# A power-of-two scale from one matmul sum of 128 maxima, and a new order table, in an attention and two-MoE kernel

## The chip, the cores and the metric

The kernel runs on one core of a Trainium2 chip. The metric is the time of one execution on the device in microseconds (us). The engines are TensorE (PE: matmuls and transposes), VectorE (DVE), ScalarE (ACT), GpSimd (POOL) and SyncE (SP, which issues the DMAs). Each engine works through its own queue in order; semaphores tie the queues together.

## The reference

Banded attention feeds a first MoE layer with a SoLU activation and a layer norm, and that feeds a bilinear MoE layer. Cut to what matters:

```python
def _attn_ref(q, k, v):                 # (4, 8, 576, 64)
    scores = scale * np.matmul(q, k.transpose(0, 1, 3, 2))
    # heads 0-3: a local band of 32; heads 4-7: every 32nd position
    attn = softmax(np.where(masks, scores, -1e9))
    return np.matmul(attn, v)

x = attn_out as (2304, 512)
h = x @ w_in                            # 512 -> 1024
solu = h * softmax(h)
ln = (solu - mu) / np.sqrt(var + 1e-06) * g_ln
x = ln @ w_out                          # 1024 -> 512
return (x @ w_a) * (x @ w_b) @ w_out2   # 512 -> 1536 -> 512
```

The inputs of the weights are float64, which the kernel turns into float32 on the chip.

## The kernel before

The work has two stages that overlap little. In the first (0 to some 290 us) PE interleaves the attention of four batches with the first MoE layer, 128 tokens a tile, 18 tiles. In the second it computes the bilinear layer in blocks of 768 tokens, as a seven-product (Strassen-like) scheme of float16 pairs, high part and low part.

**Attention.** Per pair of heads, `group_T` transposes q and k on PE into the PSUM ring `s` (L608), ACT copies them out (L615, L618). `att_tile` puts the mask and the scores into `s` (L696, L701), DVE takes the negated maximum (L719) and adds it (L728), ACT exponentiates (L731), DVE sums (L732) and takes the reciprocal (L736, L738), POOL multiplies (L777 or L768). Batch 0 is "direct": PE transposes the result into `y` (L764), ACT copies it as `PT` (L774), and P@V (L798) uses float32 values. Batches 1 to 3 split P and V into float16 high and low parts (P: L784, L785; V: `group_v`, L644 on ACT and L647 on DVE), transpose P by DMA (L786), and do P@V in three passes (L803 to L805). P@V writes the PSUM tile `xbank`, from which ACT copies to `xT` (L825).

**The values' scale.** Before V is split, it is scaled by a power of two. `pair_scale` takes for each of two head pairs the largest absolute value of every partition (L630, DVE, into a column of `am`) and calls `pow2_scale`: PE transposes `am` into `xbank` (L500), DVE reduces (L501), PE transposes the two maxima (L505), DVE reduces (L506), three tiny DVE ops make the power of two and its inverse in one row (L511 to L513), PE broadcasts the row to all partitions by a matmul with ones (L515), and DVE multiplies by units (L516). This runs six times, twice in each of batches 1 to 3. `scale_wout` uses the same function once for w_out (eight columns), and the second stage three times.

**The shared bank.** `xbank` is one PSUM tile of 512 columns. P@V uses the columns up to 352 as ring `x`, the scale those from 352 on as ring `scp`. The two rings know nothing of each other in the plan, but the program's semaphores follow the tile as a whole: a transpose of the scale waits for ACT's copy out of it, and P@V for the scale's last reads.

**The first MoE layer.** `moe1(t)`: ACT and DVE split a slice of `xT` into `xh` and `xl` (L845, L849), PE makes `h` in 24 matmuls (L856), DVE takes the maximum (L861), ACT exponentiates (L862), POOL makes a reciprocal (L867 to L869), DVE multiplies (L871, into `wk`), and the rest (L875 to L890) normalises. `h` is one PSUM buffer, so tile t+1 cannot start before L871 of tile t. `s2` multiplies by `wout` (L910) into `y`. The weights come as float64, 512 KB a piece, and are converted by ACT and DVE (`from_f64`, L455, L461, L465); `split_wout` (L524, L526) needs the scale of w_out. `scale_ab` (L929) sums norms by a matmul of a 128x128 block of ones by two columns.

**The order.** `Plan.op` collects operations with engines, costs in microseconds, and dependences; `schedule` puts them out in the order of the table `ISSUE`, which was found beforehand by a search that reads these costs and the rings' buffers. Within an engine the table's order is the queue's order, and no engine passes over a waiting instruction. The costs are read by the search alone.

## Time and profile before

| | us |
|---|---|
| median of 3 runs | 700.77 (699.4 to 700.79) |
| profiled execution | 695.03 |
| its span, first to last instruction | 693.3 |
| PE busy | 664.4 (96%) |
| DVE busy | 571.5 (82%) |
| ACT busy | 447.2 (65%) |
| POOL busy | 144.7 (21%) |

The mean granted clock of TensorE over the span is 0.994. The share of DMA engines busy is near 1 up to 60 us and falls afterwards. Busy times are shares over a span with different stages, so they are read by stretch. Each wait is put down to whatever came last. The rows that matter stand in a section of their own below.

### The profile page before, as it was taken

How to read it: one execution, taken by the hardware profiler on the slowest of the kernel's cores; microseconds unless marked ns; L12 is line 12 of the kernel's file. 1: busy time of each engine (PE TensorE's matmuls, PEld its weight loads, DVE VectorE, ACT ScalarE, POOL GpSimd, SP SyncE). 2: the span in 40 equal slices, each digit the busy share in tenths (PEclk: the TensorE clock that was granted, in tenths of full speed). 3: DMA queues.
4: the chain of work that ended last, by engine and by line, in shares of the span. 5: the costliest groups of instructions: out<-in, count | busy, mean ns of one | idle time of the engine just before them, and what ended most of it. 6: DMA issues, size and time to landing. Idle time of an engine off the chain costs nothing.

```text
span 693.3 us, 15572 instructions
## 1 busy us (share of the span) xinstructions
PE 664.4 (96%) x5991; PEld 498.8 (72%) x5991; DVE 571.5 (82%) x1238; ACT 447.2 (65%) x898; POOL 144.7 (21%) x268
## 2 busy tenths in 40 slices
PE   5987899999999999999999999999999999999997
PEld 4766677878787888886576676766767676775676
DVE  5789899789678644999999999799977989786576
ACT  3679868777767644986978787676543746434421
POOL 5544546536537432410000000000000000000000
PEclk9999899999999999999999999999999999999999
DMA  9999979999998434677254043653522304641023
GB/s 209 258 243 244 188 138 194 264 186 268 222 248 199 102 81 102 188 249 240 103 184 152 0 141 104 198 201 97 175 100 94 120 32 166 237 138 46 1 92 122
DMA packets 152650, 109.68 MB, mean 158 GB/s; under 512 B 101376, under 2 KB 131072, under 8 KB 152576
## 3 DMA queue, kind: packets, MB, share of 16 engines
q1 hardware_dynamic: 152576, 108.69, 60.4%
q8 instruction: 47, 0.77, 0.5%
q14 instruction: 27, 0.22, 0.1%
HBM read 65.41 MB, written 27.53 MB: 134 GB/s over the span
## 4 chain that ended last, share of the span: by engine, by line
PE 61%; DVE 8%; ACT 5%; issue 1%; POOL 0%; ACTq 0%; POOLq 0%
PE N L1326 17%; PE M L1326 13%; PE N L1472 9%; PE y L910 7%; PE M L1472 7%; PE h L856 6%; ACT y L1267 1%; DVE p L1423 1%; ACT w L1128 1%; DVE w L1132 1%; DVE y L1269 1%; DVE A L1415 1%; DVE A L1393 1%; DVE V L647 0%; ACT Z L1238 0%
## 5 line engine op out<-in xcount | busy, mean ns | idle before, releaser
L1326 PEld LDWEIGHTS <-w 128*128 128x128 f16 x1512 | 147.9, 98 | 91.7 <-issue 2.0
L1326 PE MATMUL N<-y,w 128*128 128x384 f16 x864 | 156.2, 326 | 0.7 <-ACT N L1333 0.7
L1472 PEld LDWEIGHTS <-p 128*128 128x128 f16 x1071 | 104.7, 98 | 20.4 <-issue 1.1
L1326 PE MATMUL M<-y,w 128*128 128x384 f16 x648 | 118.5, 326 | 0.8 <-ACT N L1333 0.8
L910 PE MATMUL y<-lnT,wout 128*128 128x256 f16 x864 | 101.4, 273 | 1.5 <-DMA lnT<-ln 0.8
L910 PEld LDWEIGHTS <-wout 128*128 128x128 f16 x864 | 82.0, 98 | 15.2 <-issue 4.1
L1418 ACT CAST p<-A 128x384 f16<-128x384 f32 x119 | 59.2, 512 | 40.1 <-DVE A L1393 22.6
L856 PE MATMUL h<-win,xh 128*128 128x512 f32 x288 | 79.8, 417 | 2.7 <-DVE wk L871 2.6
L1472 PE MATMUL N<-wo,p 128*128 128x256 f16 x612 | 77.7, 273 | 1.0 <-DVE yst L1488 1.0
L856 PEld LDWEIGHTS h<-win,xh 128*128 128x128 f32 x288 | 54.4, 198 | 14.4 <-DVE wk L871 3.3
L1423 DVE TENSOR_TENSOR p<-A,p 128x384 f16<-128x384 f32 x119 | 62.3, 552 | 2.7 <-ACT p L1418 2.7
L1472 PE MATMUL M<-wo,p 128*128 128x256 f16 x459 | 60.2, 273 | 0.0
L455 ACT ACTIVATE f64f<-raw 128x512 f32<-128x512 f32 x52 | 34.6, 674 | 11.2 <-DMA raw<-in_moe_w_in_dram 7.3
L856 PE MATMUL h<-win,xl 128*128 128x512 f32 x144 | 39.2, 394 | 0.0
L1415 DVE TENSOR_TENSOR A<-A 128x384 f32<-128x384 f32 x72 | 39.0, 553 | 0.2
L1488 DVE SCALAR_TENSOR_TENSOR ob<-M,osc,ob 128x256 f32<-128x256 f32 x63 | 27.8, 477 | 12.6 <-PE M L1472 11.1
L777 POOL TENSOR_TENSOR e<-e,r 128x324 f32<-128x324 f32 (+2 forms) x30 | 26.2, 881 | 50.0 <-DVE r L738 28.2
L861 DVE TENSOR_REDUCE st<-h 128x1 f32<-128x1024 f32 x18 | 22.0, 1220 | 17.2 <-PE h L856 17.1
L856 PEld LDWEIGHTS h<-win,xl 128*128 128x128 f32 x144 | 26.7, 188 | 5.9
L465 DVE SCALAR_TENSOR_TENSOR f64f<-f64f,raw 128x512 int32<-128x512 int32 x36 | 28.8, 804 | 2.3 <-ACT f64f L455 1.8
L1348 ACT COPY V<-M 128x384 f32<-128x384 f32 x36 | 17.0, 473 | 20.0 <-PE M L1326 19.9
L871 DVE SCALAR_TENSOR_TENSOR wk<-h,st,wk 128x1024 f32<-128x1024 f32 x18 | 23.0, 1279 | 7.8 <-POOL st L869 7.7
(191 smaller groups left out, 1207.0 us busy)
## 6 DMA issues: line engine op xcount, KB each, us to landing
raw<-in_moe_w_out_dram SPq DMA_DIRECT2D x20, 512.0 KB
o_scr<-ob SPq DMA_DIRECT2D x36, 256.0 KB
ob<-o_scr SPq DMA_DIRECT2D x30, 256.0 KB
raw<-in_moe_w_a_dram SPq DMA_DIRECT2D x12, 512.0 KB
raw<-in_moe_w_b_dram SPq DMA_DIRECT2D x12, 512.0 KB
y_scr<-y SPq DMA_DIRECT2D x14, 384.0 KB
y<-y_scr SPq DMA_DIRECT2D x14, 384.0 KB
y_scr<-ys SPq DMA_DIRECT2D x18, 256.0 KB
```

The costliest lines, as they stand in the source:

```text
L455: act(0.67, lambda: nc.scalar.activation(f(), raw()[:, :, 1].bitcast(F32), AF.Prelu, scale=2.0 ** -112, alpha=-2.0 ** 32), (raw,), (f,))
L465: dve(0.77, lambda: nc.vector.scalar_tensor_tensor(g().bitcast(I32), f().bitcast(I32), 3, raw()[:, :, 0], op0=ALU.logical_shift_left, op1= ...
L777: pool(0.1 + 1.2 * pl, lambda: nc.gpsimd.tensor_tensor(ev(), ev(), r()[:, :ng].unsqueeze(2).to_broadcast([128, ng, nk]), op=ALU.mult), (r, ...
L856: nc.tensor.matmul(h()[:, 512 * n:512 * n + 512], xs[xa]()[:, kk], win[wa][:, kk, 512 * n:512 * n + 512], start=(pi == 0 and kk == 0), sto ...
L871: dve(1.3, lambda: nc.vector.scalar_tensor_tensor(e(), h(), st()[:, 7:8], e(), op0=ALU.mult, op1=ALU.mult, accum_out=st()[:, 2:3]), (h, (s ...
L910: nc.tensor.matmul(y()[:, 256 * mi:256 * mi + 256], wout[:, kk, wa, 128 * m:128 * m + 128], lnT()[:, xa, kk], start=(pi == 0 and kk == 0), ...
L1326: nc.tensor.matmul(to()[:, :HB], w()[:, wa, a, kk], y7[b]()[:, xa, kk], start=first and pi == 0 and kk == 0, stop=pi == 2 and kk == 1, ski ...
L1415: dve(TD, lambda: nc.vector.tensor_tensor(to(), x(), y(), op=op), toks, (to,))
L1418: act(0.5, lambda: nc.scalar.copy(pu(0, a), x()), (x,), (pu.tok(0, a),))
L1423: dve(TD, lambda: nc.vector.tensor_tensor(pu(1, a), x(), pu(0, a), op=ALU.subtract), (x, pu.tok(0, a)), (pu.tok(1, a),))
L1472: nc.tensor.matmul(bk(i), pus[u](xa, a)[:, 128 * tt:128 * tt + 128], wo()[:, u, b, wa], start=a == A11 and u == 0 and pi == 0, stop=u == U ...
L1488: dve(0.475, lambda: nc.vector.scalar_tensor_tensor(dst(), bk(i), s(), dst(), op0=ALU.mult, op1=ALU.add), (src, osc), (obt(t, c),))
```

## The change

Five things change.

1. `pair_scale` no longer calls `pow2_scale`. It multiplies a 128x128 block of ones by each column of `am`, adding up in one PSUM column (`total`): every partition then holds the sum of all 128 maxima of both head pairs instead of the largest. DVE masks the sum to its exponent (one op on 128x1), and `powers` makes the inverse and the scale in three ops on 128x1.
2. Ring `scp` is gone. `x` is the whole of `xbank`, one buffer, which P@V, the values' scale and the scale of w_out take in turn; the plan therefore orders them.
3. `scale_wout` keeps its seven steps, but takes its tile from `x` (`scp="x"` in `PARAM`).
4. Costs of PE operations that the search reads are raised.
5. The table `ISSUE` is a new one: 3237 operations instead of 3261, with rows moved on every engine.

```diff
-PARAM = dict(back=12, first=40, early=(0,), seed=4, noise=0.1, direct=((0, 0), (0, 1)), stay=0.0, pf1=(),
+PARAM = dict(scp="x", back=12, first=40, early=(0,), seed=4, noise=0.1, direct=((0, 0), (0, 1)), stay=0.0, pf1=(),
 ISSUE = [int(n) for n in """
-10 0 13 11 14 5 2 15 16 1 12 6 18 17 21 8 35 19 9 20 7 4 22 414 37 430 3 771 787 36 39 38 40 43 41 42 181 187 23 66 44
+10 0 13 5 14 2 15 1 11 16 12 6 17 18 20 8 35 21 9 19 414 7 4 22 426 3 763 37 775 36 39 38 40 43 41 42 181 187 24 23 66
...
-    ring("psR", "x", None, F32, 1).fixed = lambda n: xbank[:, :352]
-    ring("psR", "scp", None, F32, 1).fixed = lambda n: xbank[:, 352:]
+    ring("psR", "x", None, F32, 1).fixed = lambda n: xbank
...
-    def pow2_scale(am, toks, n, unit, dst, dtok, top=14, least=60, ps="scp", sm=""):
-        tp = bank(ps) if ps == "M" else rings[ps].new()
+    def pow2_scale(am, toks, n, unit, dst, dtok, top=14, least=60, ps=None, sm=""):
+        tp = bank(ps) if ps == "M" else rings[ps or pm["scp"]].new()
-        pe(0.12, lambda: nc.tensor.transpose(tp()[:n, :128], am(), ident), (*toks, "ident"), (tp,))
+        pe(0.2, lambda: nc.tensor.transpose(tp()[:n, :128], am(), ident), (*toks, "ident"), (tp,))
...
-        pe(0.1, lambda: nc.tensor.matmul(tp()[:, 144:146], ones, row()[:1], start=True, stop=True), (row, "small"), (tp,))
+        pe(0.25, lambda: nc.tensor.matmul(tp()[:, 144:146], ones, row()[:1], start=True, stop=True), (row, "small"), (tp,))
...
-            pe(NM * 0.09, transposes, ((raw, 0), (raw, 1), "ident"), (tp,), 855)
+            pe(NM * 0.09 + 0.05, transposes, ((raw, 0), (raw, 1), "ident"), (tp,), 855)
...
-        pow2_scale(am, (am,), len(gs), 0, sc, sc)
+        tp, m1 = rings["x"].new(), rings["m1"].new()
+
+        def total():
+            for i in range(len(gs)):
+                nc.tensor.matmul(tp()[:, :1], ones_sq, am()[:, i:i + 1], start=i == 0, stop=i == len(gs) - 1)
+        pe(0.3, total, (am, "small"), (tp,))
+        dve(0.15, lambda: nc.vector.tensor_scalar(m1().bitcast(I32), tp()[:, :1].bitcast(I32), 0x7F800000, None,
+                                                  op0=ALU.bitwise_and), (tp,), (m1,))
+
+        def powers():
+            up, down = sc()[:, 0:1], sc()[:, 1:2]
+            nc.vector.tensor_scalar(down, m1(), 2.0 ** -14, 2.0 ** -60, op0=ALU.mult, op1=ALU.max)
+            nc.vector.reciprocal(up, down)
+            nc.vector.tensor_scalar(down, down, 1.0 / PSCALE, None, op0=ALU.mult)
+        dve(0.4, powers, (m1,), (sc,))
...
-            pe(nblk * 0.14, transposes, (tok, "ident"), (pt,), nblk * rows * 2)
+            pe(nblk * 0.15 + 0.05, transposes, (tok, "ident"), (pt,), nblk * rows * 2)
...
-                s1_ops.append(pe(4 * 0.230, mm, [xs[xa]] + [((("win", kk, n), wa)) for kk in range(4)], (h,), 2048))
+                s1_ops.append(pe(4 * 0.237, mm, [xs[xa]] + [((("win", kk, n), wa)) for kk in range(4)], (h,), 2048))
...
-        pe(0.12, lambda: nc.tensor.matmul(tp()[:, :2], ones_sq, fro[:, u, m], start=True, stop=True),
+        pe(0.22, lambda: nc.tensor.matmul(tp()[:, :2], ones_sq, fro[:, u, m], start=True, stop=True),
```

Three places show how the queues change. Line numbers of the new kernel differ: L635 is the matmul of `total`, L637 DVE's masking of the sum, and L499 to L514 are the old L501 to L516 shifted by two; L883 is the old L871 (eviction of `h`), L873 the old L861, L888 the old L876, L868 the old L856.

On DVE, the last rows ahead of the eviction of `h` of MoE tile 1. Before:

```order
L736 SCALAR_TENSOR_TENSOR sm_927<-sm_927,over 128x6
L465 SCALAR_TENSOR_TENSOR wout<-f64f,raw_797 128x512
L461 TENSOR_SCALAR raw_869<-raw_869 128x512
L738 RECIPROCAL r<-sm_927 128x6
L861 TENSOR_REDUCE st<-h 128x1
L465 SCALAR_TENSOR_TENSOR wout<-f64f,raw_869 128x512
L732 TENSOR_REDUCE sm_1013<-e_116 128x6
L849 TENSOR_TENSOR xl<-xT,xh 128x512
L719 TENSOR_REDUCE mx<-s 128x6
L871 SCALAR_TENSOR_TENSOR wk,st<-h,st,wk 128x1024
```

The same place in the changed kernel:

```order
L888 SCALAR_TENSOR_TENSOR ln<-wk,st,ln 128x1024
L873 TENSOR_REDUCE st<-h 128x1
L504 TENSOR_REDUCE m_1086<-xbank 1x1
L744 TENSOR_REDUCE sm_1088<-e_114 128x6
L509 TENSOR_SCALAR m_1086<-m_1086 1x1
L510 TENSOR_SCALAR row<-m_1086 1x1
L511 RECIPROCAL row<-row 1x1
L861 TENSOR_TENSOR xl<-xT,xh 128x512
L744 TENSOR_REDUCE sm_1111<-e_115 128x6
L514 TENSOR_TENSOR wsc<-xbank,units 128x2
L748 SCALAR_TENSOR_TENSOR sm_1088<-sm_1088,over 128x6
L883 SCALAR_TENSOR_TENSOR wk,st<-h,st,wk 128x1024
```

The steps of the scale of w_out, which stood behind this eviction, now stand ahead of it. From one eviction to the next (tile 0 to tile 1) 18 DVE rows stood between, now 32 instructions do.

On PE, the first values' scale. Before, it follows the last matmuls of MoE tile 2, with its second transpose behind two groups of other work and its broadcast 20 rows further on:

```order
L856 MATMUL h<-win_108,xl 128x512 x4
L608 MATMUL s<-ident,rawq 128x96 x6
L500 MATMUL xbank<-ident,am 2x128
L798 MATMUL xbank<-PT,rawl 64x64 x2
L608 MATMUL s<-ident,rawk 128x96 x6
L505 MATMUL xbank<-ident,m_1184 1x2
L696 LDWEIGHTS identb
```

In the changed kernel, both values' scales of batch 1:

```order
L606 MATMUL s<-ident,rawq 128x96 x6
L513 MATMUL xbank<-row,ones 128x2
L635 MATMUL xbank<-am,ones 128x1 x2
L868 MATMUL h<-win_108,xh 128x512 x4
L868 MATMUL h<-win_109,xh 128x512 x4
L868 MATMUL h<-win_108,xl 128x512 x4
L868 MATMUL h<-win_108,xh 128x512 x4
L635 MATMUL xbank<-am,ones 128x1 x2
L868 MATMUL h<-win_109,xh 128x512 x4
```

Three visits of PE with DVE between them have become one; the first follows the broadcast of the scale of w_out and stands ahead of tile 2, the second amid tile 2. The P@V of tile 8 of batch 0 that stood here (L798) has moved ahead.

On ACT, the start of the program. Before:

```order
L615 ACTIVATE qkT<-s 128x2x16x18
L455 ACTIVATE f64f<-raw_252 128x512
L455 ACTIVATE f64f<-raw_254 128x512
L774 COPY PT<-y 128x384
L474 CAST win_108<-f64f 128x512
```

In the changed kernel:

```order
L613 ACTIVATE qkT<-s 128x2x16x18
L453 ACTIVATE f64f<-raw_252 128x512
L786 COPY PT<-y 128x384
L453 ACTIVATE f64f<-raw_254 128x512
L472 CAST win_108<-f64f 128x512
```

The copy of the first transposed tile (`PT`) has moved ahead of the second weight conversion.

## Rows read from the trace of the kernel before

**Rows 1.** Stretches: window, length, PE, PEld, DVE, ACT, POOL busy (instructions), clock, DMA.
```profile
60.00:124.00 64.00, 57.16 (x768) 45.42 (x767) 60.40 (x140) 49.72 (x96) 36.42 (x59) 0.95 1.01 181
124.00:290.00 166.00, 163.81 (x1802) 134.28 (x1800) 120.70 (x235) 114.13 (x207) 74.02 (x149) 1.00 0.85 189
290.00:440.00 150.00, 147.77 (x1079) 104.86 (x1077) 146.82 (x316) 120.17 (x245) 5.08 (x9) 1.00 0.43 143
```
**Rows 2.** Waits of PE, whole span: who waited <- for whom: total us, times, longest.
```profile
PE h L856 <- DVE wk L871: 2.6, 3, 2.0
...
PE xbank L505 <- DVE m L501: 1.1, 2, 0.7
PE xbank L500 <- DVE sc L516: 1.0, 2, 0.5
...
PE xbank L803 <- DVE sc L516: 1.0, 2, 0.6
...
PE xbank L515 <- DVE row L513: 0.5, 1, 0.5
```
**Rows 3.** Waits of DVE from 60 to 124 us.
```profile
DVE m L501 <- ACT xT L825: 1.5, 1, 1.5
DVE m L501 <- PE xbank L805: 1.2, 1, 1.2
```
**Rows 4.** Lines of the scale (ns min/median/max), and pieces of the chain (start, us).
```profile
L501 DVE TENSOR_REDUCE m<-xbank x7: 238/270/279, 72.9 to 184.5; 2x1 f32<-2x128 f32 x6, 8x1 f32<-8x128 f32 x1
L506 DVE TENSOR_REDUCE m<-xbank x7: 115/146/154, 73.7 to 187.8; 1x1 f32<-1x2 f32 x6, 1x1 f32<-1x8 f32 x1
L511 DVE TENSOR_SCALAR m<-m x7: 109/141/142, 73.9 to 188.0; 1x1 int32<-1x1 int32 x7
L516 DVE TENSOR_TENSOR sc<-xbank,units x6: 113/140/159, 85.2 to 215.1; 128x2 f32<-128x2 f32 x6
L515 PE MATMUL xbank<-row,ones x14: 237/246/267, 74.7 to 207.7; 1*128 1x2 f32 x14
L935 DVE TENSOR_SCALAR small<-small x12: 153/154/156, 205.7 to 541.3; 128x1 int32<-128x1 int32 x12
183.91 0.27 PE xbank L500
187.67 0.09 PE xbank L505
205.00 0.31 PE y L929 x2
```
**Rows 5.** Timelines of PE, then DVE, near tile 2: start, us, instruction, [idle before].
```profile
57.04 2.11 PE L856 MATMUL h<-win,xh 128*128 128x512 f32 x8 [0.45 <-DVE wk L871]
64.75 0.72 PE L608 MATMUL s<-ident,rawq 96*128 96x96 f32 x6
67.44 3.64 PE L856 MATMUL h<-win,xh 128*128 128x512 f32 x8 [1.97 <-DVE wk L871]
60.24 0.48 DVE L732 TENSOR_REDUCE sm<-e 128x6 f32<-128x324 f32 x1
66.10 1.28 DVE L871 SCALAR_TENSOR_TENSOR wk<-h,st,wk 128x1024 f32<-128x1024 f32 x1
74.46 1.30 DVE L630 TENSOR_REDUCE am<-rawl 96x1 f32<-96x1152 f32 x1
```
**Rows 6.** One slice behind that idle time, columns as in rows 1.
```profile
68.00:70.00 2.00, 2.00 (x6) 1.57 (x5) 1.97 (x6) 2.00 (x6) 0.98 (x2) 0.50 0.78 118
```
**Rows 7.** Timelines of ACT, then PE, at the start.
```profile
14.88 0.69 ACT L455 ACTIVATE f64f<-raw 128x512 f32<-128x512 f32 x1 [2.62 <-DMA raw<-in_moe_w_in_dram]
16.75 0.66 ACT L455 ACTIVATE f64f<-raw 128x512 f32<-128x512 f32 x1 [1.17 <-DMA raw<-in_moe_w_in_dram]
17.31 0.46 ACT L774 COPY PT<-y 128x384 f32<-128x384 f32 x1
17.91 0.87 PE L764 MATMUL y<-ident,e 128*128 128x128 f32 x3 [2.44 <-ACT PT L774]
```

More of the change, by code (lines that the diff above doesn't have):

```diff
@@ L704, in att_tile @@
         if not (g.strided and j):
-            pe(2 * npb * nk * 0.42e-3 + sum(4 * kk / 2.4e3 + 0.01 for kk in groups) + 0.03, scores,
+            pe(2 * npb * nk * 0.42e-3 + sum(4 * kk / 2.4e3 + 0.01 for kk in groups) + 0.1, scores,
                ((g.T, 0), (g.T, 1), "identb", "masks" if g.strided else "maskl"), [(sp, f) for f in range(2)],
@@ L806, in att_tile @@
         if direct:
-            pe(sum(4 * c[5] / 2.4e3 + (0.06 if g.strided else 0.015) for c in cells if not c[0]), pv, (PT, *g.vtoks), (x,),
+            pe(sum(4 * c[5] / 2.4e3 + (0.06 if g.strided else 0.015) for c in cells if not c[0]) + 0.07, pv, (PT, *g.vtoks), (x,),
                1.3 * sum(2 * c[5] * nk / 128 for c in cells), 1)
         else:
-            pe(sum(3 * c[5] / 2.4e3 + (0.035 if g.strided else 0.015) for c in cells if not c[0]), pv, (PT, *g.V), (x,),
+            pe(sum(3 * c[5] / 2.4e3 + (0.035 if g.strided else 0.015) for c in cells if not c[0]) + 0.07, pv, (PT, *g.V), (x,),
                1.27 * sum(1.5 * c[5] * nk / 128 for c in cells), 1)
```

261 rows, old and new, of the table ISSUE are left out of this document.

## The prediction

> **What bounds the kernel now.** I read the stretches first, because the share of busy time over the whole span mixes stages. From 124 us on TensorE (PE) is the bound: it is busy for 163.81 of 166 us up to 290, and for 147.77 of 150 us up to 440 [rows 1]. There a microsecond of PE waiting is a microsecond of the kernel. Between 60 and 124 us it is another engine: VectorE (DVE) is busy for 60.40 of 64 us while PE has 57.16 [rows 1]. What PE can do there hangs on how early DVE hands things over. Before 60 us the kernel waits for loads and for the first chains.
>
> Next, what PE waits for. The scale chain costs it 1.1 us before L505, 1.0 before L500, 1.0 before P@V (L803, which waits for the scale's last step), and 0.5 before L515; the eviction of h by DVE (L871) costs 2.6 [rows 2]. So 3.6 us of PE's waits carry the scale's name. Last, what DVE itself waits for between 60 and 124 us: 1.5 us for the wout scale, whose first transpose stands behind the ACT copy out of the shared bank, and 1.2 us for a values' scale whose transpose stands behind P@V in the bank [rows 3]. These 2.7 us are most of the 3.6 us that DVE is idle there.
>
> **The values' scale: waits that go.** Six chains of PE, DVE, PE, DVE, PE, DVE become PE, DVE. In the PE-bound part the waits named for the scale are the L515 one (0.5), one of the L500 ones and one of the L803 ones; halving the two-times rows of 1.0 gives 0.5 each, 1.5 together [rows 2]. What is next late in their place: the sum of maxima still needs the two maxima of DVE, and P@V still needs V, which needs the scale. The new chain is two steps long, so I take -1.4 us, between -1.5 and 0.
>
> **Its instructions on PE.** Removed per pair: 0.27 us of transpose, 0.09 of the second transpose and about 0.25 of the broadcast, 0.61 us [rows 4]. Added: two matmuls of a 128x128 float32 block of ones by one column. The trace of before has none; the nearest is L929, the same block by two columns, whose one call held the chain of work for 0.31 us, as two records [rows 4]. Two calls cost at most 0.62, and at least the 0.09 of the smallest PE step there. I take 0.43, the upper half, since each call is again two records. That is -0.18 per pair, three pairs in the PE-bound part: -0.5 us (0 to -1.6). In the DVE-bound part it is hidden behind DVE.
>
> **Its instructions on DVE.** Removed per pair: 0.270 + 0.146 + 3 x 0.141 + 0.140 = 0.98 us [rows 4]. Added: four ops on 128x1, priced by L935, a 128x1 op of 0.154 us: 0.62 [rows 4]. That is -0.36 us per pair. Three pairs stand before 124 us, where DVE is the bound: -1.1 us. The values' wait of 1.2 us in DVE goes with the chain. The wout scale keeps its seven steps; its 1.5 us may go, since it now has other DVE work around it, or come back. I count it as staying. The stretch from 60 to 124 us gives -1.1 - 1.2 = -2.3 us, between -3.8 (the wout wait gone too) and -1.1.
>
> **The order: what moved on DVE.** This is the term that works against the change. Tile 2 of the first MoE cannot start until DVE has evicted tile 1 from h. That wait is in the trace: PE is free after the transposes at 64.75, and tile 2 starts at 67.44 after 1.97 us idle, when L871 of 66.10 is done [rows 5]. In the old order 18 DVE instructions stand between the eviction of tile 0 and that of tile 1. In the new order there are 32. The 14 more are two sums of the kind of L732 (0.48) and two additions over as many elements (L728, taken at the same 0.48), one maximum over raw values (1.30), six of the wout scale (0.98 together), and three small ones of some 0.14 [rows 4, 5]: 1.92 + 1.30 + 0.98 + 0.42 = 4.6 us, and about 4 us where neighbours overlap. The wout scale among them must also go to PE and back twice before DVE can reach the eviction. Against this PE gets more to do meanwhile: three more groups of transposes and scores and the scale's own steps, some 3 us by the 0.7 us of such a group [rows 5]. So tile 2 starts 4 to 6 us later with 3 us more work behind it: a loss of 1 to 3 us, 5 us at worst. It is partly given back: from there to the eviction of tile 3, 54 DVE rows follow instead of 75, and tile 4 stands earlier on PE. I take +2 us, between 0 and +5.
>
> The clock belongs here. After the idle time before tile 2 the granted clock falls to 0.50, which is the lower of the two levels, 1.2 GHz, in the slice from 68 to 70 us [rows 6]; the eight matmuls that take 2.11 us for tile 1 take 3.64 us for tile 2 [rows 5]. So a dip costs 1.5 us of PE. Before has it already, so I add nothing; a second dip would be 1.5 more. The Trainium skill, TensorE: Matmul & The Clock Gate, section on the HAM clock gate, says that the throttled clock is the default and that activity releases it; by that rule a longer hole before tile 2 speaks against this order, and the sum would be 1.5 us higher. The trace agrees on the two levels; whether the longer hole costs a longer dip no run here shows yet.
>
> **The start.** On ACT the first copy of PT moves ahead of the second weight conversion, which waited for its load until 16.75; PE lost 2.44 us at 17.91 to that copy [rows 7]. That copy began at 17.31 and could begin behind the first conversion, which runs from 14.88 to 15.57, so up to 1.8 us could be won there. But on DVE a conversion that waits for the same load now stands ahead of the next scores' maxima, and the first MoE tile still needs all eight converted pieces of w_in, which come at the pace of the loads. I take 0 (-1.8 to +1).
>
> **From 290 us on** nearly the same work runs in nearly the same order. PE waits for 2.2 us there and DVE is busy for 146.82 of 150 us [rows 1], so moved rows may cost or give about 1 us; I take 0. The table's new costs (0.2 for 0.12 and the like) are read only by the search and take no time themselves. The loads move by a few places in SP's queue; I add nothing for them.
>
> **The sum:** -1.4 - 0.5 - 2.3 + 2.0 = -2.2 us. On the profiled execution's 695.03 us (a span of 693.3 and 1.7 around it) that is 692.8. The median of the runs shown is 5.7 us above the profiled one, and nothing in the trace says where that lies, so I carry the difference over: 700.77 - 2.2 = 698.6 us.
>
> **The rivals.** A measurement of this kernel can tell about 0.2% from no change, 1.4 us.
>
> First, the gains cancel: the later eviction costs 3 to 4 us, or P@V, which now shares one buffer with the scale, waits for DVE's masked read of the sum behind DVE's own queue, up to 0.5 us per pair as L500 did [rows 2]. Then the change does not do what it says, it only renames the wait: -1.4 - 0.5 - 2.3 + 4 = -0.2, 700.6 us. For it: DVE is full where this happens. Against it: the chain has four steps fewer. 0.2.
>
> Second, slower: the eviction of tile 1 behind the wout scale. Place: DVE between 57 and 75 us. Price: 5 us for the eviction, 1.5 for a longer dip of the clock, and the 1.2 us on DVE not won because DVE now waits for PE elsewhere: -1.4 - 0.5 - 1.1 + 5 + 1.5 = +3.5, 704.3 us. It decides where the later start of tile 2, less the 3 us of work done meanwhile, passes the 4.2 us of the gains: a start 7.2 us later, or 5.7 us with the longer dip. For it: the 14 rows are counted, not guessed, and PE is full after 124 us, so nothing absorbs a loss. Against it: the 21 rows fewer afterwards. 0.3.
>
> Third, the start pays too and the wout wait vanishes: -1.4 - 1.0 - 3.8 + 1 - 1.8 = -7.0, 693.8 us. It is the good end of the forecast, not a case of its own.
>
> **How the numbers follow.** 0.5 for the forecast (faster by more than 1.4 us), 0.2 for no change, 0.3 for slower. The likeliest case alone is 693.5 to 699.3. As the slower case holds 0.3, the range reaches through it to 704.3: 693.5 to 704.3.
>
> **What would show it.** In the new profile: no chain of L501 to L516 for the values; PE's waits before the sum of maxima under 1 us in all; DVE idle under 2.5 us between 60 and 124. The idle time before tile 2 should grow from 1.97 to 3 to 5 us, and tile 4, which begins at 110 us now, should start some 4 us earlier. If tile 4 starts no earlier, the rows were not given back and the slower case holds. The prediction is wrong on its main term if PE is not full by 124 us, or if a new wait above 1 us on the shared bank appears.

## The result, and the profile after

The changed kernel takes 705.7 us (median of 4 runs, 704.19 to 706.86); the kernel before, run beside it, 700.09. The ratio is 1.0085, 95% interval 1.0061 to 1.0109: some 6 us slower. The forecast was 698.6 us and faster; the result lies above its range, which ended at 704.3. The profiled execution took 705.62 us, with a span of 703.8 and a mean granted clock of 0.970 (before: 0.994).

The stretches of after, columns as in [rows 1], with the first 60 us added:

```profile
0.00:60.00 60.00, 42.54 (x536) 34.39 (x537) 43.63 (x99) 36.53 (x74) 27.72 (x53) 0.77 1.01 242
60.00:124.00 64.00, 57.40 (x742) 46.52 (x740) 60.18 (x125) 50.52 (x99) 39.05 (x59) 0.95 1.02 194
124.00:290.00 166.00, 161.11 (x1791) 131.70 (x1792) 111.63 (x228) 107.86 (x196) 68.92 (x145) 0.98 0.78 175
290.00:440.00 150.00, 146.45 (x1043) 103.04 (x1042) 146.09 (x310) 121.53 (x240) 8.43 (x11) 1.00 0.46 151
```

PE was to be full from 124 us on. It is idle for 4.9 us of the 166 (2.2 before) and for 3.6 of the 150 behind (2.2 before). The low clock of the first 60 us (0.77) belongs to the execution, as the unchanged kernel shows further on.

Who keeps PE waiting, whole span of after, columns as in [rows 2] (three larger rows, of 7.2, 4.6 and 3.6 us, are left out; all but 1.3 us of them lies in the first 60 us):

```profile
...
PE h L868 <- DVE wk L883: 2.7, 3, 2.0
PE y L922 <- DMA lnT<-ln: 1.7, 1, 1.7
...
PE M L1338 <- ACT N L1345: 1.4, 1, 1.4
...
PE M L1484 <- ACT V L1360: 0.9, 1, 0.9
...
PE xbank L503 <- DVE m L499: 0.6, 1, 0.6
PE M L1338 <- DVE y L1281: 0.6, 1, 0.6
...
PE xbank L635 <- DVE wsc L514: 0.5, 1, 0.5
```

Of the 3.6 us that carried the scale's name in [rows 2], 1.1 are left, and both are the scale of w_out (L503, and L635 behind `wsc`). The values' scale has no wait of PE in this list. The change does what it says. But other waits have grown or moved. The eviction of `h` costs as much in all as before (2.7 against 2.6), but its longest wait, 2.0 us, stood ahead of tile 2 and now stands ahead of tile 5, where PE was to be full. A transposed `ln` costs 1.7 instead of 0.8 us, and three rows of the second stage add up to 2.9.

By tile, as first matmul of the tile on PE, before and after: tile 2 at 67.4 and 74.2 us, tile 4 at 110.4 and 106.5, tile 10 at 198.7 and 205.7, tile 17 at 282.0 and 289.4. From tile 17 to PE's end it is 407.9 and 411.1. Tile 4 is 4 us early, as forecast, this seems lost again, with more, between tiles 4 and 10, and another 3.2 us go behind 290 us.

Most of that lead is no gain. The start of a tile tells little where other work is moved across them: ahead of tile 4 PE runs 508 matmuls into `s` and 104 into `y` in after, 566 and 128 in before; from tile 4 to tile 10 it is the other way, 364 and 314 against 312 and 288. In the executions at full clock PE is busy from tile 4 to 10 for 83.9 to 85.6 us with the old order throughout the first stage and 88.8 to 90.3 with the new. So some 5 us of work were put off, not saved. At tile 17 the counts are level again, and there the times can be compared.

**The wait at tile 5.** POOL, DVE and PE of after, and POOL and DVE of before, at the eviction of tile 4 (start, us, instruction, [idle before]):

```profile
115.52 0.75 POOL L789 TENSOR_TENSOR e<-e,r 128x324 f32<-128x324 f32 x1 [1.23 <-DVE r L750]
117.13 2.30 POOL L789 TENSOR_TENSOR e<-e,r 128x324 f32<-128x324 f32 x1 [0.86 <-DVE r L750]
119.39 1.96 POOL L797 TENSOR_TENSOR P<-e,P 128x324 f16<-128x324 f32 x2
121.43 0.24 POOL L879 TENSOR_SCALAR st<-st 128x1 f32<-128x1 f32 x1
...
117.55 1.28 DVE L463 SCALAR_TENSOR_TENSOR f64f<-f64f,raw 128x512 int32<-128x512 int32 x2
118.76 1.21 DVE L873 TENSOR_REDUCE st<-h 128x1 f32<-128x1024 f32 x1
...
122.73 1.28 DVE L883 SCALAR_TENSOR_TENSOR wk<-h,st,wk 128x1024 f32<-128x1024 f32 x1 [2.01 <-POOL st L881]
...
124.17 2.47 PE L868 MATMUL h<-win,xh 128*128 128x512 f32 x8 [2.04 <-DVE wk L883]
```
```profile
118.77 0.60 POOL L867 TENSOR_SCALAR st<-st 128x1 f32<-128x1 f32 x1 [1.65 <-DVE st L861]
...
120.54 1.27 DVE L871 SCALAR_TENSOR_TENSOR wk<-h,st,wk 128x1024 f32<-128x1024 f32 x1
```

Before, POOL waited for DVE's maximum and began the reciprocal as soon as it was there. Now the maximum is ready at 119.97 (118.76 and 1.21), but POOL, whose multiply ended only at 119.43, is still at two operations on `P` that stand ahead in its queue, and starts at 121.43. DVE waits 2.01 us for POOL, and PE 2.04 us for DVE.

POOL is late also because one multiply took 2.30 us where the same one took 0.75 two microseconds earlier; the long one runs beside DVE's L463, which reads two tiles. The Trainium skill (GPSIMD Engine Reference, section 1, Specifications) says that GpSimd shares its SBUF interfaces with VectorE and meets contention from DVE instructions with two SBUF inputs. These rows agree. Over all 20 traces the same multiply takes 0.72 to 0.76 us in each of the 176 places where no such DVE operation runs beside it, and 1.60 us or more in the 18 places where such operations run beside it for over 0.9 us. One run further on, tile4_early, moves the DVE rows away from it.

**The second stage.** PE of after, near 350 us; before there was one wait of 0.83 us here:

```profile
349.96 1.46 PE L1338 MATMUL M<-y,w 128*128 128x384 f16 x8 [0.56 <-DVE y L1281]
352.83 4.06 PE L1338 MATMUL M<-y,w 128*128 128x384 f16 x24 [1.41 <-ACT N L1345]
```

### The profile page after: what moved, and what is told of

It is laid out like the page before. It is cut to its first block, busy times and chain, and to the rows that moved or that the text cites. A ratio compares the mean times of both kernels' runs of the same rounds, so it can differ in the third digit from the quotient of the medians.

```text
span 703.8 us, 15569 instructions
## 1 busy us (share of the span) xinstructions
PE 666.8 (95%) x5991; PEld 499.8 (71%) x5991; DVE 569.0 (81%) x1226; ACT 447.1 (64%) x898; POOL 144.1 (20%) x268
## 4 chain that ended last, share of the span: by engine, by line
PE 50%; DVE 20%; DMA 4%; ACT 4%; issue 2%; SPq 0%; DVEq 0%; ACTq 0%
PE N L1338 12%; PE M L1338 9%; PE N L1484 8%; PE y L922 7%; PE h L868 7%; PE M L1484 6%; DMA lnT<-ln 2%; DVE p L1435 2%; DVE y L1281 2%; DVE A L1405 2%; DVE w L1144 1%; DVE A L1427 1%; DVE yst L1289 1%; DVE S L1130 1%; DVE C L1349 1%
## 5 line engine op out<-in xcount | busy, mean ns | idle before, releaser
L868 PE MATMUL h<-win,xh 128*128 128x512 f32 x288 | 80.7, 419 | 2.8 <-DVE wk L883 2.7
L868 PEld LDWEIGHTS h<-win,xh 128*128 128x128 f32 x288 | 54.4, 198 | 15.1 <-issue 2.3
L873 DVE TENSOR_REDUCE st<-h 128x1 f32<-128x1024 f32 x18 | 21.9, 1219 | 26.3 <-PE h L868 26.3
L868 PE MATMUL h<-win,xl 128*128 128x512 f32 x144 | 40.3, 403 | 0.0
L883 DVE SCALAR_TENSOR_TENSOR wk<-h,st,wk 128x1024 f32<-128x1024 f32 x18 | 23.1, 1282 | 11.3 <-POOL st L881 10.0
L868 PEld LDWEIGHTS h<-win,xl 128*128 128x128 f32 x144 | 27.4, 194 | 6.1
L1500 DVE SCALAR_TENSOR_TENSOR ob<-N,osc,ob 128x256 f32<-128x256 f32 x45 | 20.4, 481 | 13.8 <-PE N L1484 13.7
L797 POOL TENSOR_TENSOR P<-e,P 128x324 f16<-128x324 f32 (+2 forms) x30 | 28.7, 963 | 7.0 <-ACT P L796 6.8
```

What stands on the lines that cost most here:

```text
L797: pool(0.15 + 1.4 * pl, lambda: nc.gpsimd.tensor_tensor(plo, ev(), ph, op=ALU.subtract), (e, ("P2", pi, 0)), (("P2", pi, 1),))
L868: nc.tensor.matmul(h()[:, 512 * n:512 * n + 512], xs[xa]()[:, kk], win[wa][:, kk, 512 * n:512 * n + 512], start=(pi == 0 and kk == 0), sto ...
L883: dve(1.3, lambda: nc.vector.scalar_tensor_tensor(e(), h(), st()[:, 7:8], e(), op0=ALU.mult, op1=ALU.mult, accum_out=st()[:, 2:3]), (h, (s ...
L1500: dve(0.475, lambda: nc.vector.scalar_tensor_tensor(dst(), bk(i), s(), dst(), op0=ALU.mult, op1=ALU.add), (src, osc), (obt(t, c),))
```

## The experiments

All but the first use the new scale's instructions (or leave the scale out) and give P@V and the scale separate columns again; only the order differs. "Old order" is the table before, with the rows of the new scale put in for the old ones. Two orders are joined at a point of the old table: what stood ahead of it in one order, the rest in the other. Line numbers in these kernels are one higher than in the changed one (L884 for L883). A ratio of 0.001 is 0.7 us.

| kernel | order | ratio to before, 95% interval | tile 4 | tile 10 | tile 17 | from there to PE's end |
|---|---|---|---|---|---|---|
| before (profile) | old, old scale | 1 | 110.4 | 198.7 | 282.0 | 407.9 |
| before_again | the same | 1.0001 (0.9970 to 1.0031) | 114.6 | 202.7 | 286.1 | 408.2 |
| scale_only | old | 0.9999 (0.9974 to 1.0025) | 117.5 | 204.2 | 287.6 | 408.1 |
| only_again | the same | 1.0005 (0.9976 to 1.0033) | 113.6 | 201.6 | 284.9 | 408.3 |
| scale_late | old, DVE's steps later | 0.9913 (0.9877 to 0.9950) | 113.5 | 200.8 | 284.1 | 408.5 |
| late_again | the same | 0.9950 (0.9926 to 0.9975) | 111.5 | 199.4 | 283.1 | 407.9 |
| scale_last | old, later again | 0.9964 (0.9936 to 0.9992) | 111.3 | 198.1 | 281.2 | 407.8 |
| no_scale | old, constant scale | 0.9917 (0.9889 to 0.9944) | 110.2 | 197.3 | 280.7 | 408.3 |
| first_new | new to 290 us | 1.0013 (0.9986 to 1.0040) | 107.7 | 203.8 | 287.5 | 408.3 |
| tile4_early | the same, tile 4 mended | 1.0037 (1.0015 to 1.0059) | 107.9 | 204.8 | 288.4 | 408.6 |
| start_new | new to 136 us | 1.0008 (0.9987 to 1.0029) | 108.2 | 206.2 | 289.5 | 408.2 |
| mid_new | new 136 to 290 us | 1.0140 (1.0113 to 1.0167) | 117.8 | 213.6 | 297.3 | 408.3 |
| second_new | new from 290 us | 1.0045 (1.0009 to 1.0081) | 117.2 | 202.4 | 285.8 | 411.8 |
| wb_early | the same, one load mended | 1.0043 (1.0016 to 1.0070) | 114.4 | 201.2 | 284.6 | 411.4 |
| late_new | new 290 to 350 us | 1.0050 (1.0028 to 1.0073) | 117.7 | 204.5 | 287.8 | 412.2 |
| late_a | new 290 to 326 us | 1.0037 (1.0012 to 1.0062) | 116.7 | 203.3 | 286.6 | 411.1 |
| late_b | new 326 to 350 us | 1.0072 (1.0049 to 1.0095) | 116.1 | 202.9 | 286.3 | 412.1 |
| order_new_sep | new | 1.0085 (1.0052 to 1.0118) | 106.9 | 201.0 | 284.7 | 412.6 |
| new_noscale | new, constant scale | 1.0153 (1.0116 to 1.0189) | 109.9 | 205.1 | 288.5 | 413.6 |
| changed kernel | new, shared buffer | 1.0085 (1.0061 to 1.0109) | 106.5 | 205.7 | 289.4 | 411.1 |

The last four columns, in us, are of one profiled execution each, and up to tile 17 executions of one kernel differ by some 4 us (before and before_again). The last column does not scatter: with the old order behind 290 us it is 407.8 to 408.6 in twelve executions, with any part of the new one 411.1 to 413.6 in eight.

### Scale or order, first or second stage

> The kernel before, unchanged, profiled a second time. Its first profile (695.03 us) lies below all four timed runs (697.65 to 700.79) and shows two short stretches at half clock, both after 67 us, while the changed kernel's profile has long ones between 20 and 50 us. If the first 60 us of the old order also meet such stretches in some executions, this profile is 698 to 701 us and shows a clock below 1.00 before 60 us. If the half clock at the start belongs to the new order alone, this profile is again near 695 us with a clock of 1.00 up to 60 us. The ratio to the kernel before is 1.000 within 0.003 either way.

It measured no difference (1.0001), as it must. Its profile settles the clock of the first 60 us: 0.80 with the old order too. Its first two stretches:

```profile
0.00:60.00 60.00, 42.14 (x535) 33.83 (x536) 41.71 (x98) 36.34 (x71) 29.50 (x53) 0.80 1.02 236
60.00:124.00 64.00, 57.30 (x745) 44.92 (x744) 57.79 (x130) 49.65 (x97) 32.26 (x51) 0.92 0.92 174
```

> The new values' scale alone: the sum of 128 maxima and the four 128x1 DVE ops, put where the first transpose and the first reduction stood; the old order for everything else, and the two separate rings in the shared bank. Theory one (the new order costs, the scale itself pays): 1 to 4 us faster than before, 697 to 699.5 us, with no PE wait on L505 or L515 of the values and less of the 3.6 us of scale waits. Theory two (the scale itself costs, because P@V now waits for DVE's masked read): 2 to 6 us slower, with new PE waits on the shared bank.

The edit to the changed kernel, beside the table of the order:

```diff
-PARAM = dict(scp="x", back=12, ...
+PARAM = dict(scp="scp", back=12, ...
...
-    ring("psR", "x", None, F32, 1).fixed = lambda n: xbank
+    ring("psR", "x", None, F32, 1).fixed = lambda n: xbank[:, :352]
+    ring("psR", "scp", None, F32, 1).fixed = lambda n: xbank[:, 352:]
...
-        tp, m1 = rings["x"].new(), rings["m1"].new()
+        tp, m1 = rings["scp"].new(), rings["m1"].new()
```

> The new scale with separate rings; the new order for all operations up to the last first-layer matmul of MoE tile 17 (some 290 us), the old order behind that. Theory A (the loss lies between 124 and 290 us, where the profile after falls back 5 to 6 us by waits at 175 to 185 us and a stretch at half clock): 703 to 706 us, as slow as the changed kernel or up to 3 us better. Theory B (the loss lies from 290 us on): 697 to 700 us.

> The new scale with separate rings; the old order up to the last first-layer matmul of MoE tile 17 (some 290 us), the new order behind that. Theory A: 697 to 701 us, no worse than 1 to 2 us over the scale alone. Theory B (the loss lies from 290 us on, where PE waits for 3.6 us in the profile after and for 1.5 before): 701 to 704 us, 3 us or more over the scale alone.

The new scale alone gives nothing (0.9999), where the sum had -4.2 us. Against that, the new order up to 290 us adds about 1 us, which is within the noise (1.0013), the new order behind 290 us 3 us (1.0045). So the loss that shows is where the prediction had put zero. (Against the later places of the scale's steps, further on, the first stage loses too.) What the new scale meets in the old order shows in DVE's waits from 60 to 124 us of scale_only:

```profile
DVE st L874 <- PE h L869: 3.0, 2, 2.6
DVE m L638 <- PE xbank L818: 2.9, 1, 2.9
```

DVE's masking of the sum (L638) had been put where the old chain's first reduction stood. The 2.9 us stand at the second values' scale (in only_again, the same kernel, 2.4 us, at the same place):

```profile
98.19 0.50 PE L636 MATMUL xbank<-am,ones 128*128 128x1 f32 x4
...
100.02 0.16 DVE L638 TENSOR_SCALAR m<-xbank 128x1 int32<-128x1 int32 x1 [2.87 <-PE xbank L818]
```

The sum's matmuls stand in PE's queue behind P@V and a matmul group of the first layer. They are done at 98.69, but the masking begins at 100.02: its wait is put down to L818, the last pass of the next P@V in the same bank, which ends at 99.39.

### Is the chain worth anything?

> The old order with separate columns, but the values' scale is a constant: the two matmuls of the sum, the masking and the three ops of the powers are left out and two memsets of the two columns stand in their place (the maxima over the values are still taken). This bounds what any change to the chain can gain. Theory A (as in the prediction's sum: the chain costs PE its waits and DVE its rows, some 4 us): 694 to 696.5 us, ratio to before 0.991 to 0.995. Theory B (the chain is covered, what PE and DVE wait for next comes just as late): as with the new scale alone, ratio 0.998 to 1.001.

The edit, beside the table without the rows left out:

```diff
-        pe(0.3, total, (am, "small"), (tp,))
-        dve(0.15, lambda: nc.vector.tensor_scalar(m1()...
...
+            nc.vector.memset(sc()[:, 0:1], 32.0)
+            nc.vector.memset(sc()[:, 1:2], 0.03125 / PSCALE)
+        dve(0.1, powers, (), (sc,))
```

It gave 0.9917, 5.8 us: in the old order the chain is not covered, and what a change to it can win is there to be had.

> The old order and the new scale in separate columns, but DVE's masking of the sum stands where the second reduction stood, and the powers where the power of two was made, and no longer both at the place of the first reduction, where VectorE waited 2.9 us for P@V. If that wait ate the gain of the scale: VectorE waits under 0.5 us for the sum between 60 and 124 us, and 1 to 3 us are won, 696 to 699 us, ratio 0.994 to 0.998. If the chain is covered anyway: the wait goes, the time stays, ratio 0.998 to 1.001.

The edit is one of the order alone. DVE in scale_late against scale_only, first values' scale (the masking that waited 2.9 us is the second, moved likewise):

```diff
-L638 TENSOR_SCALAR m_1185<-xbank 128x1
-L643 TENSOR_SCALAR sc<-m_1185 128x1
+L862 TENSOR_TENSOR xl<-xT,xh 128x512
+L525 SCALAR_TENSOR_TENSOR wout<-wout,gs_sb 128x512
+L638 TENSOR_SCALAR m_1201<-xbank 128x1
+L625 MEMSET am 128x2
+L460 TENSOR_SCALAR raw_957<-raw_957 128x512
+L884 SCALAR_TENSOR_TENSOR wk,st<-h,st,wk 128x1024
+L525 SCALAR_TENSOR_TENSOR wout<-wout,gs_sb 128x512
+L643 TENSOR_SCALAR sc<-m_1201 128x1
```

Ratio 0.9913. DVE's waits of 60 to 124 us in scale_late:

```profile
...
DVE st L874 <- PE h L869: 1.5, 2, 1.1
...
DVE m L638 <- ACT xT L838: 0.6, 1, 0.6
```

The wait of L638 fell from 2.9 to 0.6 us (under 0.5 was expected).

> As the kernel with the old order and the new scale whose DVE steps stand behind the first reduction's place, but a step later again: the masking of the sum where the power of two was made and the powers where the broadcast was read. If the gain is that of the chain's length (fewer rows on VectorE and TensorE, no wait for the bank): again 0.989 to 0.994. If it hung on V being ready earlier than before: V is as late here as in the kernel before, and the ratio goes back to 0.997 to 1.001.

Again faster, 0.9964, with no wait of L638 in the list of DVE's waits at all; so the gain does not hang on the scale being ready as early as in scale_late. On V itself the run says little: DVE's part of V for the second scale begins at 104.1 us here and in late_again alike. To settle that the two places differ, and not two groups of runs, both kernels ran once more side by side on one chip:

> The kernel with the old order and the new scale, its masking and powers on VectorE at the later places, on one chip beside the one at the first reduction's place. If the place of these rows is what decides: ratio to before 0.989 to 0.996, and 2 us or more below its neighbour. If the difference between the two came from different chips and groups of runs: within 1 us of its neighbour.

> The kernel with the old order and the new scale, its masking and powers on VectorE together at the place of the old first reduction. If the place decides: ratio to before 0.998 to 1.002, 2 us or more above its neighbour. If not: within 1 us of it.

0.9950 against 1.0005, medians of 696.12 and 700.4 us: 4.3 us apart. The later place is what lets the shorter chain pay. This version, old order and new scale with DVE's steps later, beats both kernels: by 3.5 and 6.1 us (its two ratios) the one before, and, ratio against ratio, by 9 to 12 us the changed one.

### The order, by place

> The changed kernel with its new order throughout, but P@V and the scale in separate columns of the bank again. If the shared buffer itself costs nothing and only the order does: the time of the changed kernel, 704 to 706.5 us, ratio 1.006 to 1.010. If the shared columns cost a wait of P@V for the masking of the sum: 702 to 703.5 us.

1.0085, the changed kernel's own ratio: to within some 3 us (the two intervals) sharing the buffer costs nothing by itself; the order does. With the same instructions, the new order stands 0.0135 to 0.0172 above the old one with the late masking (1.0085 less 0.9950 and 0.9913): those are the 9 to 12 us. Some 4 of them lie behind tile 17 (412.6 against 407.9 and 408.5), the rest, by subtraction, ahead of it.

> The new order throughout, but the values' scale is a constant (the sum's matmuls, the masking and the powers left out, two memsets in their place). If the changed kernel is slow because its order makes the scale chain late: 4 to 6 us are won against the changed kernel, as in the old order, 699 to 702 us, ratio 0.999 to 1.003. If the loss is that of the other moved rows, with the chain already covered there: 703 to 706 us, ratio 1.005 to 1.009.

Neither theory had this: without the chain the new order is no faster, and by its ratio slower still, 1.0153 (the interval only just touches that of 1.0085, from another chip). So the chain is not what makes the changed kernel slow, and in this order its absence wins nothing. Why less work takes longer there isn't settled.

> New scale in separate columns; the new order up to the first matmul of MoE tile 6 (about 136 us), the old order behind. Theory A (the order's effects are local and add up): the gain that the trace of the changed kernel shows by tile 4 (2.5 to 3.7 us) stays, 695 to 697 us, ratio to before 0.993 to 0.997. Theory B (what is won by tile 4 is given back at tiles 7 to 9 whatever the order there, since loads and the DMA transposes of ln set the time): no gain, 698 to 701 us, ratio 0.998 to 1.002.

> New scale in separate columns; the old order up to the first matmul of MoE tile 6, the new order from there to the last first-layer matmul of tile 17 (136 to 290 us), the old order behind. Theory A: the loss between tiles 7 and 9 (4 to 7 us in the traces of the new order) is of the order there: 702 to 706 us, ratio 1.004 to 1.009. Theory B: without the earlier gain there is little to give back: 698 to 701 us, ratio 0.998 to 1.002.

The theory of effects that add up falls. The early start alone wins nothing (1.0008): tile 4 is early at 108.2 us, but as in the changed kernel with fewer matmuls ahead of it (508 into `s` and 104 into `y`), and at the next tiles the lead is given back. The middle alone costs 10 us (1.0140), while start and middle together, first_new, cost 1. A part of this may be the seam at 136 us, where two orders meet that weren't made for each other; in mid_new PE waits 2.7 and 2.8 us right behind it. PE of start_new behind tile 4, then two slices of the same execution:

```profile
126.48 2.72 PE L869 MATMUL h<-win,xh 128*128 128x512 f32 x8 [2.10 <-DVE wk L884]
```
```profile
124.00:130.00 6.00, 3.90 (x15) 2.94 (x13) 3.61 (x5) 4.29 (x8) 1.72 (x6) 0.81 0.83 280
136.00:146.00 10.00, 9.47 (x128) 7.41 (x116) 7.71 (x23) 6.11 (x12) 4.62 (x10) 0.66 0.90 214
```

The 2.1 us at tile 5 and the low clock of the two slices (0.19 of 6 and 0.34 of 10 us, up to 4.5 us of PE at full speed) are more than could have been won. The wait at tile 5 is not the seam's: it stands, with 1.2 to 2.2 us, in every execution with the new start.

> The kernel with the new order up to 290 us and the old behind, with three steps of MoE tile 4 moved ahead: its maximum on VectorE ahead of three rows of a weight's conversion, its exponential on ScalarE ahead of four rows, its reciprocal on GpSimd ahead of two multiplies of P. In every trace with the new start, VectorE's eviction of tile 4 waited 2 us for that reciprocal and PE 2 us for the eviction. Either way PE's wait before tile 5 should fall from 2.1 to under 0.5 us. If that wait is where the gain of the start goes: 697 to 699 us, ratio 0.996 to 0.999. If something else is as late (loads, the transposes of ln at tiles 7 to 9): no change, ratio 1.000 to 1.002.

POOL's edit, against first_new (DVE's maximum and ACT's exponential are moved likewise):

```diff
-L798 TENSOR_TENSOR P_2_107<-e_116,P_2_107 128x6x54
-L798 TENSOR_TENSOR P_0_105<-e_114,P_0_105 128x6x54
 L880 TENSOR_SCALAR st<-st 128x1
 L881 TENSOR_SCALAR st<-st 128x1
 L882 TENSOR_TENSOR st<-st,small 128x1
+L798 TENSOR_TENSOR P_2_107<-e_116,P_2_107 128x6x54
+L798 TENSOR_TENSOR P_0_105<-e_114,P_0_105 128x6x54
```

A miss: 1.0037. PE of this kernel behind tile 4:

```profile
125.25 2.08 PE L869 MATMUL h<-win,xh 128*128 128x512 f32 x8 [1.23 <-DVE wk L884]
...
135.75 0.23 PE L816 MATMUL xbank<-PT,V 96*64 96x64 f16 x2 [0.86 <-ACT xT L838]
...
137.61 0.60 PE L636 MATMUL xbank<-am,ones 128*128 128x1 f32 x4 [0.71 <-ACT xT L838]
...
139.84 0.61 PE L636 MATMUL xbank<-am,ones 128*128 128x1 f32 x4 [0.40 <-DVE m L638]
```

The wait fell only from 2.1 to 1.2 us, and 2.0 us of waits stand 10 us further on, most of it for ACT's copy of `xT`. POOL and DVE of this kernel show why it did not fall further:

```profile
119.21 0.75 POOL L790 TENSOR_TENSOR e<-e,r 128x324 f32<-128x324 f32 x1 [0.86 <-DVE r L751]
120.59 2.15 POOL L880 TENSOR_SCALAR st<-st 128x1 f32<-128x1 f32 x1 [0.63 <-DVE st L874]
...
120.76 1.28 DVE L464 SCALAR_TENSOR_TENSOR f64f<-f64f,raw 128x512 int32<-128x512 int32 x2
```

The multiply that took 2.29 us in first_new takes 0.75 here, since DVE's conversion rows (L464) moved behind the maximum. But they now run beside the first step of the reciprocal (L880), which takes 2.15 us instead of 0.24. The delay went along with DVE's rows, from one POOL operation to the next. Taking half of the wait at tile 5 away did not make the kernel faster.

### The second stage

> New scale in separate columns; the old order to 290 us, the new order from there to matmul group 27 of the first products (about 350 us), the old order behind. In the trace with the new order behind 290 us PE waits 2 us more between 320 and 350 us and 1.3 us more from 410 to 500. If the first lot is of the order in that stretch: 2 us over the new scale alone, 700 to 701 us, ratio 1.002 to 1.004. If the loss is one of the whole second stage (VectorE full, a backlog that is handed on): under 1 us over the new scale alone, ratio 0.999 to 1.001.

The first 60 us of the new order here are enough for all of the loss (1.0050, and 412.2 from tile 17 to the end).

> The old order to 290 us and the new order behind, with the conversion of one piece of w_b (one row of ScalarE, two of VectorE, one of its norms) and the load that takes its buffer back at their old places, some 10 us earlier. With the new order VectorE, which is full there, waited 1.0 us for that load, and PE 2.9 us in all between 325 and 351 us. If that is the cause: PE waits under 2 us there, and the ratio falls from 1.0045 to 1.001 to 1.003. If the loss is spread over the other moved rows: the load's wait goes, PE's waits stay, ratio 1.004 to 1.006.

DVE of second_new, waiting for the load of w_b, and PE near 350 us in second_new, then in wb_early:

```profile
322.60 0.43 DVE L460 TENSOR_SCALAR raw<-raw 128x512 int32<-128x512 int32 x1 [1.01 <-DMA raw<-in_moe_w_b_dram]
...
331.95 1.14 PE L1339 MATMUL N<-y,w 128*128 128x384 f16 x6 [0.71 <-DVE C L1350]
...
347.01 1.46 PE L1339 MATMUL M<-y,w 128*128 128x384 f16 x8 [0.56 <-DVE y L1282]
349.88 4.06 PE L1339 MATMUL M<-y,w 128*128 128x384 f16 x24 [1.41 <-ACT N L1346]
```
```profile
345.19 1.46 PE L1339 MATMUL M<-y,w 128*128 128x384 f16 x8 [0.56 <-DVE y L1282]
348.06 4.06 PE L1339 MATMUL M<-y,w 128*128 128x384 f16 x24 [1.41 <-ACT N L1346]
```

The load's wait went, and with it PE's waits at 328 and 332 us; the two waits near 347 us, the ratio (1.0043) and the 411.4 us stayed. The load is not the cause.

> New scale at the first reduction's place, the old order, and the new order only from the last first-layer matmul (about 290 us) to matmul group 14 of the first products (about 326 us). The stretch 290 to 350 us in the new order cost 3 to 5 us over the new scale alone. If the early part (conversions of w_a and w_b, the first y loads) is the cause: ratio 1.003 to 1.006 and over 3 us from tile 17's start to the end more than the 408.2 of the new scale alone. Otherwise 0.999 to 1.002 and under 1 us.

> The same with the new order only from group 14 to group 27 of the first products (about 326 to 350 us). If the later part (the products' copies on ScalarE, the second y loads, the small steps of the norm between them) is the cause: ratio 1.003 to 1.006, over 3 us more than 408.2 from tile 17's start to the end. Otherwise 0.999 to 1.002 and under 1 us.

Either part alone costs as much as both: 1.0037 and 1.0072. In late_b one wait holds it, with the lower clock behind it (4.06 us of matmuls take 5.74):

```profile
350.38 5.74 PE L1339 MATMUL M<-y,w 128*128 128x384 f16 x24 [2.71 <-ACT N L1346]
```

So neither part carries the loss alone. With the old order DVE is busy for 97% of this stretch (58.14 of 60 us in scale_only), and with either part's rows moved the copies of `N` come late for PE. PE's idle time from tile 17 to its end is 3.1 to 3.8 us with the old order and 4.8 to 6.6 with the new, in the mean 2.2 us of a loss of 3.8. Which rows do it stays open, and a seam can add to it here too.

## Why the prediction was wrong, point by point

**In short.** Two terms of the sum failed. The gains of -4.2 us were taken as won whatever the order, and in the new order they are not there: with the whole chain left out it is no faster (1.0153). And the stretch from 290 us on, put at 0 (±1) because the work is nearly the same, cost 3 to 5 us. Without the gains and with the 3.2 us of second_new the sum is -2.2 + 4.2 + 3.2 = +5.2, against +5.6 measured. That the books close so well is partly luck, since the +2.0 in them was never measured by itself.

**The instructions of the scale: right.** In the traces one sum takes 0.36 to 0.47 us of PE, from its start to that of the next instruction (0.43 taken, the wait at 72.94 us apart). DVE's four ops take 0.61 us together (0.62 taken): 0.150, 0.145, 0.164 and 0.154.

```profile
L637 DVE TENSOR_SCALAR m<-xbank x6: 143/150/159, 76.8 to 219.0; 128x1 int32<-128x1 int32 x6
...
L642 DVE TENSOR_SCALAR sc<-m x6: 107/145/153, 77.4 to 220.4; 128x1 f32<-128x1 f32 x6
```

**The waits that go, -1.4, and DVE's -2.3: right in size, not in this order.** With the 0.5 of PE's instructions the sum was -4.2 us. Measured alone it is 0 where the masking stands too early, -2.5 to -6.1 where it stands late, and -5.8 with no chain at all. That the named rows brought it is not shown: DVE idles 5.3 and 2.6 us between 60 and 124 us in the two profiles of the late masking, 3.6 and 6.2 in the two of before. In the changed kernel the gain does not appear: DVE idles 3.8 us there, where under 2.5 was named as the sign. The sum also counted three pairs ahead of 124 us, as in the old order; in the new one two sums stand there (72.94 and 79.65 us) and four behind. Its waits for the scale [rows 3] are replaced by this:

```profile
DVE wk L883 <- POOL st L881: 2.8, 2, 2.0
```

The step that failed is that DVE's freed time was taken as won. POOL's queue, which the prediction left out, now ends last at the eviction of tile 4. That this wait is what eats the gain is not shown: tile4_early halved it and was no faster.

**The rows ahead of the eviction of tile 1, +2.0: the mechanism right.** PE near tile 2, as in [rows 5]:

```profile
68.27 0.17 PE L503 MATMUL xbank<-ident,m 8*1 8x8 f32 x1 [0.59 <-DVE m L499]
...
72.94 1.01 PE L635 MATMUL xbank<-am,ones 128*128 128x1 f32 x4 [0.47 <-DVE wsc L514]
74.23 1.22 PE L868 MATMUL h<-win,xh 128*128 128x512 f32 x2 [0.28 <-DVE wk L883]
```

From the eviction of tile 0 to that of tile 1 it is 14.7 us instead of 10.4: 4.3 us more, where 4.6 were counted and 4 taken (in all six executions with the new start 14.7 to 17.7, in fourteen with the old 10.4 to 12.9). Tile 2 starts 6.8 us later (4 to 6 expected); the other 2.5 us were there at the eviction of tile 0 already. The idle time right ahead of tile 2 is 0.28 us, not 3 to 5: PE has the other work that was counted, and its idle time from 67 us on comes in five pieces of 1.85 us together. Tile 4 starts 3.9 us earlier (4 expected), but this sign could not tell a gain, since PE has fewer matmuls ahead of tile 4, as shown above. The start and the eviction of tile 1 are in start_new too, which is as fast as before. The slower rival put the loss here, and its place was wrong: 704.3 us came close to the measurement for another reason. The longer dip of the clock came, though without the longer hole: the slices from 70 to 78 us show 0.75, 0.50, 0.50 and 0.54. But it cost nothing more: before has a second dip, from 80 to 86 us (0.76, 0.50, 0.89), which the prediction overlooked, and the mean clock from 60 to 124 us is 0.95 in both. The first two slices of after, and the middle of the second dip of before:

```profile
70.00:72.00 2.00, 1.73 (x27) 1.30 (x23) 1.93 (x7) 2.00 (x4) 1.23 (x4) 0.75 1.29 153
72.00:74.00 2.00, 1.48 (x6) 1.31 (x6) 2.00 (x5) 2.00 (x5) 1.72 (x4) 0.50 1.15 222
```
```profile
82.00:84.00 2.00, 1.78 (x19) 1.29 (x12) 1.93 (x7) 1.54 (x3) 0.79 (x2) 0.50 1.46 130
```

**"PE full by 124 us", the condition that was named: failed.** The 2.04 us at 124.17 and the 1.74 us for the transposed `ln` near 184 us stand where the sum had only gains. PE at the second, then the two slices around them, at a clock of 0.76 each:

```profile
183.69 2.72 PE L922 MATMUL y<-lnT,wout 128*128 128x256 f16 x12 [1.74 <-DMA lnT<-ln]
```
```profile
122.00:129.00 7.00, 4.96 (x16) 3.84 (x15) 4.83 (x7) 5.12 (x9) 1.39 (x6) 0.76 1.09 319
180.00:187.00 7.00, 5.10 (x95) 3.76 (x94) 6.96 (x18) 4.67 (x11) 4.84 (x10) 0.76 1.15 223
```

Having read that PE is the bound there, the prediction took PE's waits of before as the list of what could go, and did not ask which waits a new order brings: at the eviction POOL comes last now, and near 184 us the DMA of `ln`.

**From 290 us on, 0 (±1): the term that decided.** It cost 3 to 5 us in both comparisons: 1.0085 against 1.0013 with the new first stage, 1.0045 against 0.9999 with the old. Without it the result would have lain inside the range. "Nearly the same work in nearly the same order" is no reason for zero where [rows 1] show two engines at 98% side by side, with little slack for moved rows. Which of the rows do it, the runs leave open.

**The start, 0: not contradicted.** The low clock of the first 60 us is seen with the old order too. The profiled execution of before was 5 us under its median; before_again reaches tile 17 some 4 us later, so of the 7.4 us between the two profiles at tile 17 more than half is not the change's. Tile 0 starts later with the new start (46.5 to 48.9 us in six executions, 43.8 to 47.0 in fourteen with the old), but by its eviction the means are 0.4 us apart.

## What to carry to other kernels

Price the instructions and the order apart: a step that is cheaper pays only where its consumer's row stands behind the point at which its result is there, and moving one engine's rows by a few places was worth as much here as the whole new step. Where two engines are both nearly full, a new order of the same work is a cost of unknown size and not zero, so give it a range of its own and a chance of being a loss. Before an earlier start is read as a gain, count the work that stands ahead of it. And when rows are moved, list what every other queue (GpSimd and the DMA transposes too) must deliver at the next hand-over: here DVE's wait for POOL (2.0 us) and PE's for the DMA of `ln` (1.7 us) were not in the sum.

## What was not expected of the hardware

The mean granted clock of the first 60 us lies anywhere between 0.74 and 1.00 from one profile to the next, with the old start (0.74 in mid_new, 0.80 in before_again, 1.00 in before) as with the new (0.77 to 0.90). The profile that the prediction used was one of the two at 1.00; its time is 5 us under its kernel's median, while the other at 1.00, wb_early, is only 1.3 us under its own. One profile says little about the start of this kernel.

GpSimd's multiply of 128x324 elements took 0.72 to 0.76 us with no DVE operation with two inputs in SBUF beside it, and 2.30 us beside two of them. It goes the other way too: at 115.59 us in after it was DVE's 128x6 operation of 0.16 us, with two such inputs, that took 0.69 us, and the multiply beside it kept its 0.75. The smallest operations can be held up most: 0.24 us became 2.15 for a 128x1 step of GpSimd in tile4_early.
